# First 512 rows of x turned by TensorE instead of DMA, pinned Q/K weight loads, and memory, check and last output in smaller steps

## Chip, cores, metric

One core of one Trainium2 chip. The metric is the device time of one execution in microseconds (us), lowest is best. Only executions in the fast state are compared; the one exception is four single traces near the end (before_t1 to before_t3, pin_only_t1), for which the record leaves the state unknown and whose granted clocks (0.997 to 0.999) are those of the others. Where a "slow run" of the kernel before is spoken of below, one of its longer executions is meant (1263 us and more), which is in the fast state all the same.

Names: PE is TensorE (matmuls), PEld its weight loads, DVE is VectorE, ACT is ScalarE, POOL is GpSimd, SP is the engine whose queue issues most DMAs. "Turning" a tile means transposing it.

## The reference, cut to what matters

Two independent parts, laid side by side in the output (2048 rows, 1024 + 1024 columns, bf16).

```python
# Part A: a diagonal complex recurrence over 2048 steps between two dense projections
Bu = x @ B_bar.T            # complex, 1024 x 1024
h[t] = Lam_bar * h[t-1] + Bu[t]
y = 2 * real(hseq @ C.T) + x * Dskip

# Part B: attention in 64 segments of 32 rows, with 8 memory rows carried on
for s in range(64):
    h = concat([mem, x[32*s : 32*s+32]])       # 40 rows
    q, k, v = h @ Wq, h @ Wk, h @ Wv           # 32 heads of 128
    o = softmax(mask(q @ k.T) / sqrt(128)) @ v @ Wo
    mem, out[s] = o[:8], o[8:]
```

Part B needs x with its features on the partitions, as `b_xe` (128 partitions, 8 chunks of features, rows of x). The kernel guesses the memory rows instead of running the segments in series, computes everything at once, and checks the guess near the end. All this is the same before and after.

## The kernel before: what the change touches

The first rows of x are brought in turned, by DMA transposes on the SP queue, in pieces between the pieces of the first V weights:

```python
b.load_wv_part(w0, 0, 0, 128, nc.scalar)
b.load_xp(64, 0, 128)             # dma_start_transpose, 128 rows of x into b_xe
b.load_xp(64 + 128, 128, 128)
b.load_wv_part(w0, 0, 128, 256)
b.load_wv_part(w0, 0, 256, 512)
b.load_xp(64 + 256, 256, 128)
b.load_xp(64 + 384, 384, 128)
wv = {0: w0, 1: b.load_wv(1)}
b.load_x(1)                        # rows 512 to 1023, one DMA transpose
...
loads = [lambda: a.load_x(1), lambda: b.load_x(2), lambda: a.load_x(2),
         lambda: b.load_x(3), lambda: a.load_x(3)]   # one before each of the next V blocks
```

The first V block multiplies the four tiles of 128 rows by the first 512 columns of Wv, then copies four PSUM banks to `b_vst`, alternately on DVE and ACT, and stores `b_vst` into the DRAM tensor `b_vx`. There are two `b_vst` buffers, so a V block may only be copied out when the store of the block before the last one has landed.

```python
for i, c0, c1 in ((0, 0, 128), (1, 0, 128), (0, 128, 256), (1, 128, 256),
                  (0, 256, 512), (1, 256, 512), (2, 0, 512), (3, 0, 512)):
    self.v_mm(ps[i], w, i, c0, c1)
```

In this stage the order of PE and SP is pinned to the program's order. DVE, ACT and POOL have no pin: there the build places instructions where it expects them to fit.

```python
G.affine_select(out=k.fmask[:, 0, :], ...)     # POOL
G.memset(k.fmask[0:M, 0, :], 1.0)              # POOL
V.tensor_scalar(k.fmask[:, 1, :], k.fmask[:, 0, :], 1.0, 1.0e9, ALU.subtract, ALU.mult)   # DVE
```

## Time and profile before

| | before |
|---|---|
| time at the prediction | 1260.4 us, three runs 1260.22 to 1263.92 |
| execution that was traced | 1263.59 us (span 1261.9) |
| PE busy | 1240.1 us, 98% |
| DVE, ACT, POOL busy | 53%, 21%, 22% |

The page of the kernel before: its span, its busy line (busy us, share of the span, instructions) and the lines of the chain of waits that ended last.

```profile
span 1261.9 us, 19979 instructions
...
PE 1240.1 (98%) x8206; PEld 660.1 (52%) x8278; DVE 667.7 (53%) x1244; ACT 262.1 (21%) x629; POOL 273.8 (22%) x407
...
PE psP L62 9%; DVE c_ss L780 0%; PE psR L62 0%; DVE b_ost L89 0%; ACT b_ost L87 0%
...
```

PE is nearly always busy and the chain holds hardly anything but matmuls (it goes back only to 1145 us, hence the 9%). A microsecond is won only where PE idles or runs at half clock. The PE timeline shows where. Columns: start, duration, engine, line, operation, output and inputs, shape, count; in brackets the idle time before it and who ended it.

```profile
...
5.31 0.62 PE L62 MATMUL psP<-b_wv,b_xe 128*128 128x128 bf16 x8 [0.45 <-DMA b_xe<-in_B_x_dram]
6.61 0.62 PE L62 MATMUL psP<-b_wv,b_xe 128*128 128x128 bf16 x8 [0.68 <-DMA b_xe<-in_B_x_dram]
7.81 1.60 PE L62 MATMUL psP<-b_wv,b_xe 128*128 128x128 bf16 x16 [0.58 <-DMA b_wv<-in_B_Wv_dram]
...
15.82 0.18 PE L62 MATMUL psR<-ident,a_r 24*128 24x24 bf16 x1
16.76 0.34 PE L62 MATMUL psR<-ident,b_xr 8*128 8x8 bf16 x8 [0.76 <-DVE a_raw L168]
17.03 19.21 PE L62 MATMUL psP<-b_wv,b_xe 128*128 128x512 bf16 x86
36.81 1.89 PE L62 MATMUL psP<-b_wv,b_xe 128*128 128x512 bf16 x8 [0.57 <-ACT b_vst L87]
...
43.65 7.08 PE L62 MATMUL psP<-b_wv,b_xe 128*128 128x512 bf16 x31 [1.50 <-DMA b_xe<-in_B_x_dram]
...
```

The first three V pieces wait for DMA. `a_raw` and `b_m0` (16.76) share one PSUM bank, psR. At 36.81 PE waits for an ACT copy, and at 43.65 for the DMA transpose of block 2 of x.

The full timeline of the same trace around 350 us:

```profile
...
338.17 1.60 POOL L300 DMA_DIRECT2D a_xn<-in_A_x_dram  x3
...
341.25 0.37 ACTq L470 DMA_DIRECT2D b_vx<-b_vst  x1
...
344.39 0.38 SPq L62 DMA_DIRECT2D b_wq<-in_B_Wq_dram  x1
344.87 1.21 SPq L62 DMA_DIRECT2D b_wk<-in_B_Wk_dram  x1
...
351.80 1.58 ACT L87 ACTIVATE b_vst<-psP 128x512 bf16<-128x512 f32 x3 [6.26 <-DMA b_vx<-b_vst]
352.45 3.18 PE L62 MATMUL psP<-b_wv,b_xe 128*128 128x512 bf16 x8 [2.37 <-ACT b_vst L87]
...
```

The ACT copy at 351.80 stood 6.26 us behind a store of `b_vx`; that store is the one issued at 341.25. PE waited 2.37 us for the copy, and its next eight matmuls took 3.18 us where eight take 1.89. Between them, SP issued the Q and K weights (1 MB). For the list of waits of all engines, one line is worth keeping in mind; it cost nothing in this kernel:

```profile
...
DVE f_mask L899 <- POOL f_mask L898: 1.8, 1, 1.8
...
```

And the end of the timeline: last DVE copy, last ACT copy, last store.

```profile
...
1255.74 0.42 DVE L89 CAST b_ost<-psP 128x256 bf16<-128x256 f32 x1 [6.42 <-PE psP L62]
1256.19 0.38 ACT L87 ACTIVATE b_ost<-psP 128x256 bf16<-128x256 f32 x1 [6.46 <-DVE b_ost L89]
1256.61 0.34 ACTq L719 DMA_DIRECT2D out_dram<-b_ost  x1
```

Below, an "excess" is a number that I worked out: the time from the start of one matmul to the start of the next, less the time that the first one streams (0.216 us for 512 columns, measured in the same trace). It includes the drain that the timeline's idle column leaves out.

### The profile page before, as it was taken

Reading aid. Unit: us, or ns where it says so; the run is one execution under the profiler, and the core shown is the slowest. Engines: PE = TensorE matmul, PEld = TensorE weight load, DVE = VectorE, ACT = ScalarE, POOL = GpSimd, SP = SyncE. Lnnn points to the kernel's source line nnn. Section 1 sums busy time; section 2 is a strip of 40 time slices with the busy share of each in tenths; the row PEclk is TensorE's granted clock in tenths of the full one; section 3 lists DMA queues with packets and bytes.
Section 4 is the critical chain, followed back from the end, with each engine's and each line's share of the span. In section 5 each row is a group of like instructions: output and inputs, shape, how many; then the busy total and the mean of one; then the engine's idle time right before and its main releaser. Section 6 shows DMA issues by size and latency. Waiting matters only on the chain. (4 is left out here: it accounts for less than half of the span.)

```text
span 1261.9 us, 19979 instructions
## 1 busy us (share of the span) xinstructions
PE 1240.1 (98%) x8206; PEld 660.1 (52%) x8278; DVE 667.7 (53%) x1244; ACT 262.1 (21%) x629; POOL 273.8 (22%) x407
## 2 busy tenths in 40 slices
PE   8999999999999999999999999999999999999997
PEld 4444444444445545656566656555566554445443
DVE  3578899998711124666666666666666641001000
ACT  4344344443310000121112121211111210000000
POOL 3111331122322220232322232232222320000000
PEclk9999999999999999999999999999999999999999
DMA  9994434554898929245464544736374279407000
GB/s 236 199 234 151 142 105 129 156 144 113 224 307 260 277 80 254 64 91 129 105 145 105 140 104 104 141 77 138 94 155 97 57 212 234 90 17 151 17 25 19
DMA packets 318536, 174.18 MB, mean 138 GB/s; under 512 B 142824, under 2 KB 304352, under 8 KB 318440
## 3 DMA queue, kind: packets, MB, share of 16 engines
q1 hardware_dynamic: 296056, 146.09, 48.8%
q10 hardware_dynamic: 21360, 23.60, 6.0%
q0 software_dynamic: 1024, 3.17, 0.8%
q8 instruction: 66, 1.08, 0.4%
q14 instruction: 30, 0.25, 0.1%
HBM read 86.42 MB, written 52.19 MB: 110 GB/s over the span
## 5 line engine op out<-in xcount | busy, mean ns | idle before, releaser
L62 PE MATMUL psP<-b_xe,b_wq 128*128 128x480 bf16 (+1 forms) x1280 | 247.8, 342 | 0.0
L62 PE MATMUL psP<-b_xe,b_wk 128*128 128x480 bf16 (+1 forms) x1280 | 247.7, 343 | 0.0
L62 PE MATMUL psP<-b_wv,b_xe 128*128 128x512 bf16 (+2 forms) x1033 | 226.7, 376 | 7.1 <-ACT b_vst L87 2.9
L614 POOL TENSOR_TENSOR b_m<-b_e,maskB 99x396 bf16<-99x396 bf16 x160 | 139.6, 872 | 337.2 <-ACT b_e L611 337.2
L611 ACT ACTIVATE b_e<-psS 99x396 bf16<-99x396 f32 x176 | 88.3, 502 | 536.8 <-PE psS L62 530.7
L62 PEld LDWEIGHTS <-b_xe 128*128 128x128 bf16 x1056 | 103.0, 99 | 128.1 <-issue 5.8
L62 PEld LDWEIGHTS <-b_wk 128*128 128x128 bf16 x1280 | 119.5, 98 | 94.4
L62 PEld LDWEIGHTS <-b_wq 128*128 128x128 bf16 x1280 | 118.8, 98 | 89.4
L89 DVE CAST b_q<-psP 128x480 bf16<-128x480 f32 (+1 forms) x192 | 98.2, 533 | 97.2 <-PE psP L62 96.2
L89 DVE CAST b_k<-psP 128x480 bf16<-128x480 f32 (+1 forms) x192 | 98.0, 532 | 95.1 <-PE psP L62 95.1
L62 PEld LDWEIGHTS <-b_ol 128*128 128x128 bf16 x832 | 81.2, 98 | 97.5
L62 PE MATMUL psU<-a_xT,a_bt 128*128 128x512 bf16 x493 | 113.9, 379 | 1.5 <-DMA a_xT<-in_A_x_dram 0.5
L62 PE MATMUL psP<-t,a_hl 128*128 128x512 bf16 x497 | 111.7, 379 | 0.8
L89 DVE CAST b_ost<-psP 128x512 bf16<-128x512 f32 (+1 forms) x17 | 11.2, 661 | 190.6 <-PE psP L62 189.5
L62 PE MATMUL psP<-t,b_ol 128*128 128x512 bf16 x408 | 91.8, 379 | 0.4
L62 PE MATMUL psP<-wo,b_ol 128*128 128x512 bf16 x407 | 91.8, 379 | 0.4
L87 ACT ACTIVATE b_vst<-psP 128x512 bf16<-128x512 f32 x126 | 72.4, 592 | 89.7 <-PE psP L62 72.4
L276 POOL TENSOR_SCALAR a_tt<-a_pr,a_tabf 128x1 f32<-128x1 f32 x48 | 34.1, 710 | 248.2 <-DVE a_pr L271 248.2
L631 DVE TENSOR_TENSOR b_ob<-psO,b_accR 99x384 bf16<-99x384 f32 x160 | 85.8, 553 | 2.5
L263 DVE TENSOR_TENSOR a_pr<-psU,a_tabf 128x2048 f32<-128x2048 f32 x32 | 73.1, 2283 | 18.6 <-PE psU L62 16.9
L62 PEld LDWEIGHTS <-a_bt 128*128 128x128 bf16 x512 | 49.2, 98 | 58.2 <-DMA a_xT<-in_A_x_dram 0.5
L62 PEld LDWEIGHTS <-a_hl 128*128 128x128 bf16 x512 | 49.2, 98 | 57.1
(192 smaller groups left out, 959.4 us busy)
## 6 DMA issues: line engine op xcount, KB each, us to landing
b_v<-b_vx SPq DMA_DIRECT2D x16, 1064.2 KB
b_wv<-in_B_Wv_dram SPq DMA_DIRECT2D x16, 1024.0 KB
b_on<-b_ob SPq DMA_DIRECT2D x15, 960.0 KB
b_vx<-b_vst ACTq DMA_DIRECT2D x24, 516.0 KB
a_hs<-a_h SPq DMA_DIRECT2D x32, 256.0 KB
b_wq<-in_B_Wq_dram SPq DMA_DIRECT2D x16, 512.0 KB
b_wk<-in_B_Wk_dram SPq DMA_DIRECT2D x16, 512.0 KB
b_wog<-in_B_Wo_dram SPq DMA_DIRECT2D x4, 2048.0 KB
```

The costliest lines, as they stand in the source:

```text
L62: r = f(*a, **kw)
L87: self.S.activation(out, in_, ACT.Copy)
L89: self.V.tensor_copy(out, in_)
L263: V.tensor_tensor(pr[:], u[:].unsqueeze(1).to_broadcast([128, 2, 2, TB]), view(t3, [[TB + 1, 2], [TB + 1, 2], [1, TB]]), ALU.mult)
L276: G.tensor_scalar(tt[:, j:j + 1], w[:, j, TB - 1:TB], t3[:, 1, TB:TB + 1], None, ALU.mult)
L611: k.S.activation(e[:], s[0:GW], ACT.Exp, scale=float(E) ** -0.5, accum_out=self.accE[0:GW, i:i + 1])
L614: k.G.tensor_tensor(m[:, 0:4 * GW].rearrange("p (a b q) -> p a b q", a=2, b=2), e[:], mask[0:GW, :, :].unsqueeze(2).to_broadcast([GW, 2, 2 ...
L631: V.tensor_tensor(self.ob[:, b0:b0 + n, :], o[0:GW, 0:n, 0:E], r.unsqueeze(2).to_broadcast([GW, n, E]), ALU.mult)
```

## The change

Intent: load the first 512 rows of x plain and turn them on PE, so that the slow DMA transposes at the start fall away; keep the Q/K weight loads from being issued too early; and break up three pieces of work on which PE waited for another engine. The core of the diff:

```diff
+    def load_x0(self, tmp, i):
+        self.x0.append(tmp.tile([128, D], BF16, name="b_xr", bufs=4))
+        self.k.SP.dma_start(self.x0[i][:], self.x[0][64 + 128 * i:192 + 128 * i, :])
+
+    def turn_x0(self, i):
+        k = self.k
+        if i % 2 == 0:
+            self.xt = k.ps("U", (128, 2, KC, 128), BF16)
+        for c in range(KC):
+            k.PE.transpose(self.xt[:, i % 2, c, :], self.x0[i][:, c * 128:(c + 1) * 128], k.ident[:])
+        for h in range(2):
+            cs = slice(4 * h, 4 * h + 4)
+            k.copy("vs"[h], self.xe[:, cs, 128 * i:128 * i + 128], self.xt[:, i % 2, cs, :])
...
-            ps = [k.ps("P")[:] for _ in range(3)] + [k.ps("U", (128, 2, 512))[:, 0, :]]
-            for i, c0, c1 in ((0, 0, 128), (1, 0, 128), ...):
-                self.v_mm(ps[i], w, i, c0, c1)
+            ps = [k.ps("P")[:] for _ in range(3)]
+            self.turn_x0(0)
+            self.turn_x0(1)
+            for i, c in ((0, 0), (0, 1), (1, 0), (1, 1)):
+                self.v_mm(ps[i], w, i, 128 * c, 128 * c + 128)
+            self.turn_x0(2)
+            self.v_mm(ps[0], w, 0, 256, 512)
+            self.v_mm(ps[1], w, 1, 256, 512)
+            self.turn_x0(3)
+            ps.append(k.ps("U", (128, 2, 512))[:, 0, :])
+            self.v_mm(ps[2], w, 2)
+            self.v_mm(ps[3], w, 3)
...
-        pm = k.ps("R")
+        pm = k.ps("U", (128, 2, 512))[:, 0, :]          # init: no longer the bank of a_raw
...
-                self.k.SP.dma_start(w[:], self.Wf[i][:, :, hp * 256:(hp + 1) * 256])
+                self.k.tc.keep_in_program_order(self.k.SP.dma_start(w[:], ...))
...
-            loads = [lambda: a.load_x(1), lambda: b.load_x(2), ...]
+            loads = [lambda: b.load_x(2), lambda: a.load_x(1), ...]
...
     # v_mem and check become generators with a yield between their PE steps:
-                if i in (27, 29):
-                    b.v_mem((i - 27) // 2, wv[(i - 27) // 2])
+                if i in (26, 28):
+                    vm = b.v_mem((i - 26) // 2, wv[(i - 26) // 2])
+                if 26 <= i < 30:
+                    next(vm)
...
+    def out_last(self, ol):          # last 128 rows: columns 512, then 256, then 256
+        ...
+            k.copy("vsv"[i], ot[:, c0:c1], p[:, 0:c1 - c0])
+            k.SP.dma_start(self.out[0, T - 128:T, D + c0:D + c1], ot[:, c0:c1])
```

Also: an early Exp on ACT, the constants (with the identity) ahead of the small parameter loads, other buffers for two small tiles, and the check between the matmuls of the third block of the output projection instead of after the second.

More of the change, by code (lines that the diff above doesn't have):

```diff
@@ L101, in consts @@
     k.hpb = c.tile([128, 1], FP32, name="hpb")
+    k.hpe = c.tile([128, 1], FP32, name="hpe")
     V.memset(k.hpb[:], HALF_PI)
+    k.S.activation(k.hpe[:], k.hpb[:], ACT.Exp)
     k.ind = c.tile([128, 4], BF16, name="ind")
@@ L355, in load_m0 @@
     def load_m0(self, tmp):
-        self.m0 = tmp.tile([M, D], BF16, name="b_xr", bufs=4)
+        self.m0 = tmp.tile([M, D], BF16, name="a_h", bufs=2)
         self.k.G.dma_start(self.m0[:], self.mem0[0])
@@ L456, in v_x @@
         if first:
-            ps = [k.ps("P")[:] for _ in range(3)] + [k.ps("U", (128, 2, 512))[:, 0, :]]
-            for i, c0, c1 in ((0, 0, 128), (1, 0, 128), (0, 128, 256), (1, 128, 256), (0, 256, 512), (1, 256, 512), (2, 0, 512), (3, 0, 512)):
-                self.v_mm(ps[i], w, i, c0, c1)
+            ps = [k.ps("P")[:] for _ in range(3)]
[10 more added lines that the diff above has]
+            self.v_mm(ps[3], w, 3)
         for i in range(4):
@@ L524, in v_mem @@
         k.copy("v", vm[:], p[:, 0:4 * NM].rearrange("p (h n) -> p h n", h=4))
+        yield
         pt = k.ps("P", (128, 1024), BF16)
@@ L532, in v_mem @@
         k.SP.dma_start(self.vt[hb][:], sv[NMX:NM, :])
+        yield
     def qk_init(self, pool):
@@ L550, in load_wqk @@
                 w = self.wq.tile([128, KC, 256], BF16, name=f"b_w{'qk'[i]}{hp % 2}", bufs=1)
-                self.k.SP.dma_start(w[:], self.Wf[i][:, :, hp * 256:(hp + 1) * 256])
+                self.k.tc.keep_in_program_order(self.k.SP.dma_start(w[:], self.Wf[i][:, :, hp * 256:(hp + 1) * 256]))
                 self.wqk[hp].append(w)
@@ L713, in out_fin @@
         t = 4 * tb + tt
-        if t == TT - 1:
-            ou = self.out[0, t * 128:(t + 1) * 128, D:2 * D]
-            for i in range(2):
-                cs = slice(half * 512 + i * 256, half * 512 + i * 256 + 256)
-                k.copy("vs"[i], osts[tt][:, cs], p[:, i * 256:i * 256 + 256])
-                (k.SP, k.nc.scalar)[i].dma_start(ou[:, cs], osts[tt][:, cs])
-            return
         k.copy("s" if half else "v", osts[tt][:, half * 512:(half + 1) * 512], p[:])
@@ L744, in outproj_first @@
             self.out_fin(p, 0, tt, half, osts)
+    def out_last(self, ol):
+        k = self.k
+        ot = self.p4a.tile([128, D], BF16, name="b_ost", bufs=4)
+        for i, (c0, c1) in enumerate(((0, 512), (512, 768), (768, 1024))):
+            p = k.ps("P")
+            for h in range(H):
+                k.PE.matmul(p[:, 0:c1 - c0], ol[h][:, 384:512], self.wo[c0 // 512][:, h, c0 % 512:c0 % 512 + c1 - c0], start=(h == 0), stop=(h == H - 1))
+            k.copy("vsv"[i], ot[:, c0:c1], p[:, 0:c1 - c0])
+            k.SP.dma_start(self.out[0, T - 128:T, D + c0:D + c1], ot[:, c0:c1])
+            yield
     def outproj(self, tb, ol):
@@ L749, in outproj @@
         for tt in range(4):
+            if 4 * tb + tt == TT - 1:
+                yield from self.out_last(ol)
+                return
             for half in range(2):
@@ L764, in check @@
             k.SP.dma_start_transpose(self.omT[:, 8 * q:8 * q + 8, :], self.tn[q][:])
+        yield
         sq = pool.tile([128, 2, KC, NM], FP32, name="c_sq", bufs=1)
@@ L782, in check @@
         V.memset(onef[:], 1.0)
+        yield
         pd = k.ps("R")
@@ L918, in warm @@
 def warm(k, pool):
-    w = pool.tile([128, 512], BF16, name="b_xr", bufs=4)
+    w = pool.tile([128, 512], BF16, name="a_n", bufs=1)
     k.V.memset(w[:], 0.0)
@@ L958, in kernel_main @@
             b.load_wv_part(w0, 0, 0, 128, nc.scalar)
-            b.load_xp(64, 0, 128)
-            b.load_xp(64 + 128, 128, 128)
-            b.load_wv_part(w0, 0, 128, 256)
-            b.load_wv_part(w0, 0, 256, 512)
-            b.load_xp(64 + 256, 256, 128)
-            b.load_xp(64 + 384, 384, 128)
+            b.x0 = []
+            for i in range(4):
+                b.load_x0(p1, i)
+                if i in (1, 2):
+                    b.load_wv_part(w0, 0, 128 * i, (256, 512)[i - 1])
             wv = {0: w0, 1: b.load_wv(1)}
             b.load_x(1)
+            consts(k)
             a.load_params(p1)
             b.load_m0(p1)
-            consts(k)
             b.stage_init()
@@ L978, in kernel_main @@
             a.tables(0)
-            loads = [lambda: a.load_x(1), lambda: b.load_x(2), lambda: a.load_x(2), lambda: b.load_x(3), lambda: a.load_x(3)]
+            loads = [lambda: b.load_x(2), lambda: a.load_x(1), lambda: a.load_x(2), lambda: b.load_x(3), lambda: a.load_x(3)]
             sx = b.sum_x(p1)
@@ L1065, in kernel_main @@
                 k.SP.dma_start(wo0[:], b.Wo[:, :, 0:512])
-            if u == 4 and hp % 2 == 0 and 2 < hp + 2 < HP:
-                b.v_mem(hp // 2 + 1)
+            if hp % 2 == 0 and 2 < hp + 2 < HP:
+                if u == 4:
+                    vm = b.v_mem(hp // 2 + 1)
+                if u in (4, 6):
+                    next(vm)
             if hp == 13 and u in (3, 6, 9):
@@ L1096, in kernel_main @@
                     k.pin.add("PE")
+                if tb == 1:
+                    ck = b.check()
+                    next(ck)
                 for n, _ in enumerate(b.outproj(tb, ol)):
@@ L1099, in kernel_main @@
                         hint(k)
-                if tb == 1:
-                    for _ in b.check():
-                        pass
+                    if tb == 2:
+                        next(ck, None)
                 ol = nx
```

## The prediction

> **What bounds the kernel.** TensorE. In the page's busy table PE is busy 1240.1 of 1261.9 us (98%), and the chain of waits that ended last is almost only matmuls. In the timeline warm 128x512 matmuls start every 0.216 us. So only PE idle time, and slow-clock time after it, can be won. From the PE start times, the gaps (us over the stream time):
>
> - head, 0 to 17: DMA waits 0.86, 0.84, 0.74, 0.44 (b_xe, b_wv); half-rate matmuls from 8.1 to 11.5; 0.91 because the one psR bank must be read (a_raw) before b_init uses it;
> - 35.9: 0.73 (ACT b_vst, held by a b_vx store); 41.8: 1.66 (DMA b_xe, block 2); 71.7: 0.60 (DMA a_xT);
> - 349.7: 2.53 (ACT b_vst, which waits 6.3 us for a b_vx store), then six matmuls at 0.41 to 0.43 us and a slow b_og: 1.7 more. The Trainium skill, "TensorE: Matmul & The Clock Gate", Part 1, says that an idle array falls to half clock; this trace agrees;
> - 464.8 and 473.7: 0.72 each (transposes of b_vm wait for its DVE copy);
> - 1022 to 1030: 1.3 (psO); 1146: 1.1 (check waits for DVE c_ss, 2.24 us);
> - tail: DVE copy 0.42, then ACT copy 0.38, then the store.
>
> **What the change saves, in us.**
>
> 1. Pinned Q/K loads: 4.0. The first pair (1 MB) is now hoisted to 344.4, when DMA moves 342 GB/s and the b_vx store of 341.25 is in flight; pinned, it goes to about 430. "DMA: Bandwidth & Descriptors", Queues, rings and completion order, says that queues share each DMA engine in turn; so the store should land some us sooner, and the gap with its half-clock tail should go.
> 2. Head: 1.0 (−0.5 to 2.5). Two 128-row DMA transposes hold the SP queue 2.9 us, the next two 4.1; plain loads about 0.5 each. The bytes are the same (2 MB by about 10 us). 32 turns at 0.056 cost 1.8 of PE, plus copies of about 0.5; smaller DMA waits pay for these. The psR wait of 0.91 goes (other bank).
> 3. SP queue some 4 us ahead, and b_xe block 2 before a_xT block 1: 1.6 at 41.8, 0.4 at 35.9 and 71.7 together. Block 2's issue should come at about 21, not 30.
> 4. Memory V in two steps: 1.4.
> 5. Check between other matmuls: 1.0.
> 6. Last output: one copy fewer in series, 0.4; 64 matmuls of 256 columns cost 0.1 more: 0.3.
> 7. Early Exp and constants: nothing, but the identity must be ready for the turns.
>
> Sum 9.7; less about 0.8 for new collisions: 8.9. All lies on PE's stream.
>
> **Prediction: 1251.5 us (1247.0 to 1257.0, 8 in 10). Faster by over 2%: 0.01; within 2%: 0.98; slower by over 2%: 0.01.**
>
> **What would show it.** PE waits: no ACT b_vst wait near 345, no half-rate matmuls there, b_wq/b_wk issued near 430 (1); second v block starting by 16 instead of 17.0 (2); no b_xe wait near 40 (3); no b_vm and c_ss waits on PE (4, 5); one copy after the last matmul (6). PE's own busy sum should hardly fall.
>
> **What would make it wrong.** Identity or x tile late: PE idles, falls to half clock and the head loses 1 to 2 us. The store at 341 limited by the 3 MB that POOL issues from 335, not by Q/K: step 1 gives under 1. A pinned weight load holding up the in-order SP queue in the attention stage: new PE waits between 500 and 1030.

## The result, and the profile after

Ratios here are the mean time of one kernel's fast runs over that of the other kernel's fast runs of the same rounds, so they are not quite the ratio of the medians quoted.

| | before | after |
|---|---|---|
| median of 4 runs | 1262.16 us | 1260.74 us |
| lowest to highest | 1260.22 to 1264.28 | 1259.40 to 1262.23 |
| ratio (95% interval) | | 0.9989 (0.9964 to 1.0013) |
| execution that was traced | 1263.59 us | 1259.40 us |

The class was foreseen (within 2%), the size was not: 8.9 us were expected, and the interval holds between 4.5 us won and 1.6 us lost. The page of the kernel after:

```profile
span 1257.7 us, 20118 instructions
...
PE 1239.0 (99%) x8270; PEld 664.0 (53%) x8342; DVE 668.2 (53%) x1248; ACT 263.7 (21%) x633; POOL 273.4 (22%) x407
...
```

PE's waits, longest in total first (columns: engine and what it wanted, who ended the wait, us in total, times, longest):

```profile
...
PE psU L62 <- ACT b_xe L87: 6.2, 2, 5.1
PE psU L62 <- DMA a_xT<-in_A_x_dram: 1.6, 1, 1.6
...
```

The waits on `b_vst`, `b_vm`, `c_ss` and `b_xe` that were to go are gone. A new one stands in front: 6.2 us for the ACT copy of a turned tile. The full timeline of the kernel after shows what is behind it:

```profile
...
9.03 0.61 PE L62 MATMUL psU<-ident,b_xr 128*128 128x128 bf16 x8
...
9.47 1.91 PE L62 MATMUL psP<-b_wv,b_xe 128*128 128x256 bf16 x16
...
15.13 0.12 POOL L936 MEMSET f_mask<- 8x40 f32 x1
15.29 0.18 DVE L937 TENSOR_SCALAR f_mask<-f_mask 40x40 f32<-40x40 f32 x1 [7.62 <-POOL f_mask L936]
15.38 0.41 DVE L89 COPY b_xe<-psU 128x512 bf16<-128x512 bf16 x1
...
15.82 0.60 ACT L87 ACTIVATE b_xe<-psU 128x512 bf16<-128x512 bf16 x1 [7.53 <-DVE b_xe L89]
...
16.47 1.01 PE L62 MATMUL psU<-ident,b_xr 128*128 128x128 bf16 x8 [5.09 <-ACT b_xe L87]
...
17.70 3.19 PE L62 MATMUL psP<-b_wv,b_xe 128*128 128x512 bf16 x7 [0.22 <-issue]
...
20.69 2.51 PE L62 MATMUL psU<-b_wv,b_xe 128*128 128x512 bf16 x8
...
```

The third turn is done at 9.64 us. Its DVE copy runs at 15.38. DVE did nothing in between: it stood at `f_mask`, which waits for the last of POOL's mask instructions (15.13). The ACT copy of that tile follows the DVE copy, the fourth turn follows the ACT copy, and PE idles 5.09 us. After that it runs at half clock: the turns start every 0.107 us instead of 0.056, and the ten matmuls from 17.70 on every 0.427 us instead of 0.216. The Trainium skill, "TensorE: Matmul & The Clock Gate", Part 1, says that an idle array falls to half clock and needs some microseconds of work to get back; this trace agrees, with 5.1 us of idling before and 5.5 us of half rate after (16.47 to 21.96). At 346 us, on the other hand, the store is no longer waited for by PE:

```profile
...
346.37 0.37 ACTq L496 DMA_DIRECT2D b_vx<-b_vst  x1
346.88 1.59 POOL L302 DMA_DIRECT2D a_xn<-in_A_x_dram  x3 [3.71 <-ACT b_vst L87]
...
353.16 1.09 ACT L87 ACTIVATE b_vst<-psP 128x512 bf16<-128x512 f32 x2 [2.50 <-DMA b_vx<-b_vst]
...
```

And the end has one copy after the last matmul:

```profile
...
1252.95 0.42 DVE L89 CAST b_ost<-psP 128x256 bf16<-128x256 f32 x1 [6.24 <-PE psP L62]
```

Following the same matmuls through both traces gives the change of each stretch:

| start of | before | after | change in the stretch |
|---|---|---|---|
| parameter matmul (end of first V block) | 15.82 | 23.13 | +7.31 |
| second V block | 17.03 | 23.44 | −0.90 |
| first block of part A | 38.53 | 44.21 | −0.73 |
| second block of part A | 50.56 | 54.57 | −1.68 |
| fourth block of part A | 72.29 | 77.41 | +1.12 |
| output projection of part A | 356.76 | 357.70 | −4.18 |
| first Q projection | 481.64 | 481.09 | −1.49 |
| last attention matmul | 1030.23 | 1028.50 | −1.18 |
| end of last matmul | 1255.70 | 1252.91 | −1.06 |
| end of span | 1261.89 | 1257.71 | −1.40 |

So in this pair of traces 12.6 us were won and 8.4 given back, 7.3 of that within the first V block.

### The profile page after: what moved, and what is told of

It is laid out like the page before. It is cut to its first block, busy times and chain, and to the rows that moved or that the text cites. A ratio compares the mean times of both kernels' runs of the same rounds, so it can differ in the third digit from the quotient of the medians.

```text
span 1257.7 us, 20118 instructions
## 1 busy us (share of the span) xinstructions
PE 1239.0 (99%) x8270; PEld 664.0 (53%) x8342; DVE 668.2 (53%) x1248; ACT 263.7 (21%) x633; POOL 273.4 (22%) x407
## 4 chain that ended last, share of the span: by engine, by line
PE 96%; POOL 1%; DMA 1%; DVE 1%; issue 1%; ACT 0%; SPq 0%; POOLq 0%; ACTq 0%; DVEq 0%
PE psP L62 80%; PE psU L62 9%; PE psS L62 3%; PE psO L62 2%; PE psR L62 2%; DMA a_xT<-in_A_x_dram 1%; POOL b_m L642 0%; DVE a_pr L273 0%; DVE a_pr L265 0%; POOL a_r L163 0%; ACT b_e L639 0%; DVE a_n L284 0%; DVE a_pr L268 0%; POOL maskB L123 0%; POOL maskA L123 0%
## 5 line engine op out<-in xcount | busy, mean ns | idle before, releaser
L62 PEld LDWEIGHTS <-b_ol 128*128 128x128 bf16 x864 | 84.2, 98 | 94.5
L62 PE MATMUL psP<-wo,b_ol 128*128 128x512 bf16 (+1 forms) x440 | 91.9, 364 | 0.4
```

The source lines that it names most:

```text
L62: r = f(*a, **kw)
```

## The experiments

Theories for the head. A: the order on DVE, where `f_mask` stands ahead of a copy on which PE now depends. B: the fourth tile of x lands late. C: two turns share one PSUM tile, so a turn waits for the copies of the turn before it by dependency alone.

The trace speaks against B already (PEld loads the fourth tile at 11.12 us), and the order as built shows how A can come about. DVE's order, counted from its first instruction, in the kernel after and in the same kernel with `f_mask` on POOL:

```
after                                   f_mask on POOL
 7 TensorCopy  b_xe<-psU                 7 TensorCopy  b_xe<-psU
 8 TensorCopy  a_jf<-a_k                 8 TensorCopy  a_jf<-a_k
 9 TensorCopy  b_xe<-psU                 9 TensorCopy  b_xe<-psU
10 TensorScalar f_mask<-f_mask          10 TensorCopy  b_xe<-psU
11 TensorCopy  b_xe<-psU                11 TensorCopy  b_vst<-psP
12 TensorCopy  b_vst<-psP               12 TensorCopy  b_xe<-psU
```

The Trainium skill, "TensorE: Matmul & The Clock Gate", in the specification table at its top, calls the queues of VectorE, ScalarE and GpSimd strict first-in first-out. This trace agrees: the copy was ready at 9.64 us and started at 15.38, right behind `f_mask`.

### e1: f_mask on GpSimd

```diff
-    V.tensor_scalar(k.fmask[:, 1, :], k.fmask[:, 0, :], 1.0, 1.0e9, ALU.subtract, ALU.mult)
+    G.tensor_scalar(k.fmask[:, 1, :], k.fmask[:, 0, :], 1.0, 1.0e9, ALU.subtract, ALU.mult)
```

> The kernel after, with the one VectorE instruction f_mask (40x40) done on GpSimd. Theory A (in-order VectorE): in the kernel after, f_mask stands in VectorE's order ahead of the b_xe copy of the third turned tile, waits for GpSimd's masks until 15.29 us and so holds the turn of the fourth tile, the first V block and its half-clock tail. Then here the 5.4 us gap of PE at 11.1 us is gone, the second V block starts at 17 to 18.5 us instead of 23.4, and the time falls by 3 to 6 us against the kernel after, so 0.993 to 0.996 of before. Theory B (the fourth x tile lands late, DMA): gap and time as in the kernel after. Theory C (the pair of turns shares one psU tile, so turn 4 waits for the copies of turn 3 by dependency alone): gap falls to about 1.3 us as between turns 1 and 2, so A and C agree here and the next run tells them apart.

Measured: 1255.33 us (1251.72 to 1259.02, 6 runs), ratio 0.9946 (0.9921 to 0.9972). In the timeline the copy of the third tile follows its turn, and the second V block starts at 17.04 us instead of 23.44:

```profile
...
11.19 0.42 DVE L89 COPY b_xe<-psU 128x512 bf16<-128x512 bf16 x1 [2.77 <-PE psU L62]
...
12.73 0.61 PE L62 MATMUL psU<-ident,b_xr 128*128 128x128 bf16 x8
...
13.40 1.67 PE L62 MATMUL psP<-b_wv,b_xe 128*128 128x512 bf16 x7
...
15.39 0.38 POOL L937 TENSOR_SCALAR f_mask<-f_mask 40x40 f32<-40x40 f32 x1
...
17.04 3.19 PE L62 MATMUL psP<-b_wv,b_xe 128*128 128x512 bf16 x14
...
```

One 40x40 instruction off DVE, and the gap of 5 us is gone. That fits A and C, not B. Of the 6.4 us won in the head the trace gives 2.1 back near 70 us: there PE waits 1.9 us for `a_xT`, and half-rate matmuls follow.

### e2: a PSUM tile for each turn

```diff
-        if i % 2 == 0:
-            self.xt = k.ps("U", (128, 2, KC, 128), BF16)
+        xt = k.ps("U", (128, 2, KC, 128), BF16)          # written and read at index 0 only
```

> The kernel after, with a psU tile of its own for each turn; f_mask stays on VectorE. Theory A: the fourth turn no longer waits, but the third block's copies still stand behind f_mask until 15.3 us and matmuls of tile 2 need them, so PE still idles some 4.5 us at 11 to 16 us and the time is within 1 us of the kernel after. Theory C: the long gap goes, the second V block starts at 17 to 18.5 us, and the time falls by 3 to 6 us. Both: the 1.3 us gap between turns 1 and 2 at 5.2 us shrinks to 0.6 or less.

Measured: 1258.86 us (1257.82 to 1259.33), ratio 0.9974 (0.9952 to 0.9995). The fourth turn runs without waiting, and then PE waits all the same, for the DVE copy itself:

```profile
...
PE psP L62 <- DVE b_xe L89: 4.6, 1, 4.6
...
```

C is out as the cause of the long gap: the wait only moved by one instruction. C does hold for the short one: the 1.14 us between the first two turns went. The time is 1.8 us below the kernel after in the same rounds (1260.62), where A expected less than 1. The chain f_mask, DVE copy, PE is the cause of the long gap.

### The two kernels again

> The kernel before itself, for noise and for a second trace. Its four runs fell in two groups, near 1260.3 and near 1264.1. If the groups are the PE gap at 349.7 us with its half-clock tail (4.2 us, waiting for a b_vx store), a run near 1260 shows no such gap, or a short one, and one near 1264 shows it. If the gap stands in both groups, they come from elsewhere (clock or start). Ratio to before 1.000 within 0.002.

> The kernel after itself, for a second trace and a narrower interval. Theory A: the gap of 5 us at 11.1 us stands in every trace, because the order on VectorE is fixed at build time. Ratio to before 0.997 to 1.000.

Measured: before against itself 1.0009 (0.9984 to 1.0034), its runs from 1259.73 to 1268.02 us. The kernel after against before 0.9987 (0.9965 to 1.0009), runs from 1258.69 to 1260.87, and the wait for ACT `b_xe` is there again (6.1 us in total). The second trace of before, of its slowest run (1268.02), has a wait of 4.1 us for `b_xe` block 2 where the first trace had 1.5, and again 2.1 us for `b_vst` near 354 us.

### e4: the kernel before, only with the Q/K loads pinned

```diff
-                self.k.SP.dma_start(w[:], self.Wf[i][:, :, hp * 256:(hp + 1) * 256])
+                self.k.tc.keep_in_program_order(self.k.SP.dma_start(w[:], self.Wf[i][:, :, hp * 256:(hp + 1) * 256]))
```

> The kernel before with nothing but the pinned Q/K loads. If the hoisted 1 MB of Q/K weights makes the b_vx store late, PE's wait for ACT b_vst near 350 us (2.5 and 2.3 us in two traces of before) goes, the eight matmuls after it start every 0.216 us, and the time falls by 4 us: 0.9968 of before (0.995 to 0.999). If the store is late because of GpSimd's 3 MB alone, the wait stays above 1.5 us and the time does not change.

Measured: 1261.43 us (1258.24 to 1264.77), ratio 0.9999 (0.9977 to 1.0022). The timed runs show no gain, and exclude 4 us. Yet the timeline shows that the pin does what it should:

```profile
...
345.16 0.37 ACTq L470 DMA_DIRECT2D b_vx<-b_vst  x1
...
353.98 1.58 ACT L87 ACTIVATE b_vst<-psP 128x512 bf16<-128x512 f32 x3 [4.54 <-PE psP L62]
354.63 1.89 PE L62 MATMUL psP<-b_wv,b_xe 128*128 128x512 bf16 x8 [0.65 <-ACT b_vst L87]
...
```

PE waits 0.65 us instead of 2.37, and the next eight matmuls take 1.89 us instead of 3.18. What was wrong with my 4 us? Both traces of before were of slow runs. So I took three more traces of before and one more of the pin alone.

> The kernel before, one more trace. Theory R (the spread of before is the wait for b_xe block 2 near 41 us alone): every trace shows the b_vst wait of about 2.3 us near 350 us, and the times differ as the wait near 41 us does (1.7 to 4.5 us). Theory S (the wait near 350 us comes and goes too): a run near 1259 to 1260 us shows less than 1 us there, and then pinning the Q/K loads gains nothing in such runs, which would explain why the timed runs of the pin alone did not fall.

> The same question of Theory R or S as for the trace beside it: does the wait for ACT b_vst near 350 us (2.3 us) stand in every run of before, or less than 1 us in its fast runs.

> The same question of Theory R or S, a third trace: does the wait for ACT b_vst near 350 us (2.3 us) stand in every run of before, or less than 1 us in its fast runs.

> The kernel before with the pinned Q/K loads alone, a second trace: wait for ACT b_vst near 350 us below 1 us and no half-rate matmuls after it, in the fast as in the slow runs; a wait for b_xe near 41 us of 0 to 4.5 us that decides the time.

| trace | time us | excess near 41 us | near 70 us | near 350 us | from 6th block of part A to its output projection |
|---|---|---|---|---|---|
| before, first | 1263.59 | 1.66 | 0.60 | 2.53 | 262.93 |
| before_again | 1268.02 | 4.30 | 1.25 | 2.26 | 262.65 |
| before_t1 | 1259.28 | none | 0.78 | 2.18 | 260.93 |
| before_t2 | 1259.74 | none | 1.60 | 2.08 | 260.83 |
| before_t3 | 1260.52 | none | 1.99 | 1.98 | 260.73 |
| pin alone | 1264.21 | 4.48 | none | 0.81 | 259.56 |
| pin alone, second | 1260.97 | none | 2.19 | 1.03 | 259.78 |
| after | 1259.40 | none | 1.72 | none | 258.76 |

The timeline of before_t1 near 350 us:

```profile
...
338.86 0.63 ACT L272 ACTIVATE a_g<-a_pr 128x512 bf16<-128x512 f32 x1
...
341.99 0.38 SPq L62 DMA_DIRECT2D b_wq<-in_B_Wq_dram  x1
...
349.06 1.58 ACT L87 ACTIVATE b_vst<-psP 128x512 bf16<-128x512 f32 x3 [5.90 <-DMA b_vx<-b_vst]
349.71 1.89 PE L62 MATMUL psP<-b_wv,b_xe 128*128 128x512 bf16 x8 [2.01 <-ACT b_vst L87]
...
```

Neither theory was quite right. The wait for `b_vst` is in every trace of before (so S falls), but the half-rate matmuls after it are only in the two slower ones: here eight matmuls take 1.89 us right after the wait. And the wait near 41 us is in the slow runs only. So Theory R is right in part: the stretch with block 2 (first to second block of part A) makes 1.7 of the 3.7 us by which the first trace is longer than the fast ones, and 6.8 of the 8.2 us of before_again, where half-rate matmuls follow the gap. The half-rate stretch after 350 us makes most of the rest (2.1 and 1.8 in the table's last column). Against the fast traces, the last column's means say that the pin alone is worth 260.83 − 259.67 = 1.2 us; against the slow ones, 3.1. The interval of the timed runs allows the 1.2 and not the 4.0.

### e8: the pin undone on a quiet base

This and the next two runs start from e6 (below): the kernel after with both repairs and earlier loads.

> The run with both repairs and the loads together, with the Q/K loads not pinned. Undoing step 1 alone on a base whose runs lie within 1.6 us. If the hoisted Q/K loads hold up the b_vx store, b_wq and b_wk are issued near 335 us, PE waits 1.5 to 2.5 us for ACT b_vst near 340 us, half-rate matmuls follow, and the time is 1252 to 1254 us. If the store is limited by GpSimd's loads alone, the time stays at 1249 to 1250.

Measured: 1249.37 us (1249.32 to 1250.26); e6, on another chip, had 1249.20, and the stretch of the table's last column takes 258.75 us in both traces. No PE wait for `b_vst`, although Q was issued at 339.19 us again (K only at 345.53, so this is half of the burst). On this base the pin is worth nothing measurable. The other thing that differs between the runs with a wait and those without is when POOL issues the 0.75 MB of `a_xn`: about 3 us ahead of the `b_vx` store in all traces with the old head (338.17 against 341.25 in the first), 0.5 us behind it in all traces with the turned head (346.88 against 346.37 in the kernel after, where POOL waited 3.71 us for an ACT copy of `b_vst`). The wait near 350 us is 0.8 to 2.5 us in the nine traces of the first kind and absent in the nine of the second. The Trainium skill, "DMA: Bandwidth & Descriptors", section on queues, rings and completion order, says that each DMA engine takes packets from its queues in turn; that a store lands sooner with less queued beside it agrees: from the store's issue to the copy that it released took 10.55 us (before), 9.04 (pin alone, second) and 6.79 (after). That the later `a_xn` is the cause was not tried by itself; why the turned head moves it is open as well.

### e5, e3, e6, e7: the head, and a version that beats both

e5 is the kernel after with the old head: DMA transposes and the old order of the first V block, all else changed.

> The kernel after with the old head (first 512 rows of x by DMA transpose, no turns); all else of the change stays, f_mask too. If the turned head is where the gain went, the first V block ends at 15.5 to 16 us, the second starts at 16 (psR wait gone), no VectorE or ScalarE wait of PE before 40 us, and the time is 1251 to 1255 us, 0.991 to 0.995 of before. If the gain was lost elsewhere (pins, load order), it stays near 0.998.

Measured: 1253.10 us (1252.26 to 1259.15), ratio 0.9944 (0.9922 to 0.9967). First V block done at 15.13 us; the second starts at 16.69, not at 16 as expected, because PE waits 1.2 us for `b_wv`. So the rest of the change gives its gain, and the turned head as written takes it back.

e3 has both repairs, `f_mask` on GpSimd and a PSUM tile for each turn.

> f_mask on GpSimd and a psU tile for each turn. Against the run with f_mask alone the PE wait of 1.2 us between turns 1 and 2 shrinks to 0.6 or less and the half-clock stretch at 6 to 10 us gets shorter; the first V block ends at 15 to 16.5 us instead of 16.7. Time 0 to 1.5 us below that run. The wait for a_xT near 70 us (2 us) stays, so part of it is given back there.

Measured: 1253.05 us (1251.53 to 1255.83), ratio 0.9937 (0.9918 to 0.9955). First V block done at 14.52 us, 2.2 us earlier than in e1 and 1.3 earlier than before; expected were 15 to 16.5. The time is 2.3 us below that of e1, but e1 ran on another chip in other rounds; by the two ratios it is about 1.1, within the 0 to 1.5 that were expected. As expected, part of it came back as a wait for `a_xT` near 70 us (2.3 us). The SP timeline of e1 shows why that load is late: it stands behind the store of `a_h`, which waits for DVE.

```profile
...
60.61 0.33 SPq L62 DMA_DIRECT2D a_hs<-a_h  x1
60.98 6.83 SPq L62 DMA_TRANSPOSE a_xT<-in_A_x_dram  x1
...
```

e6 is e3 with that load moved ahead in the program:

```diff
-loads = [lambda: b.load_x(2), lambda: a.load_x(1), lambda: a.load_x(2), lambda: b.load_x(3), lambda: a.load_x(3)]
+loads = [lambda: b.load_x(2), lambda: a.load_x(1), lambda: (a.load_x(2), b.load_x(3), a.load_x(3))]
```

> The run with both repairs, and the three DMA transposes b_xe block 3 and a_xT blocks 2 and 3 issued together, one V block earlier for the first and two for the last, ahead of the a_hs stores that wait for VectorE. If the wait for a_xT near 70 us is only the in-order SP queue standing behind those stores (the load is issued at 61 us right after one), the wait goes and the time falls 2 to 4 us below the run with both repairs: 1250 to 1253 us. If it is DMA throughput, the wait moves to 40 to 50 us and nothing is won.

Measured: 1249.20 us (1249.11 to 1250.70), ratio 0.9909 (0.9890 to 0.9928). It beats both kernels and is 3.9 us below e3 in the same rounds. The traces show where: the wait near 70 us (an excess of 2.5) is gone, and so are the half-rate matmuls behind it (from the fourth to the fifth block of part A 12.31 us in e3, 10.76 in e6). Its runs lie within 1.6 us where those of before in the same rounds spread over 6.6. PE's waits, all that are left in the span:

```profile
...
PE psR L62 <- DVE hpb L103: 1.3, 1, 1.3
PE psO L62 <- POOL b_m L641: 0.8, 3, 0.4
PE psP L62 <- ACT b_xe L87: 0.2, 1, 0.2
```

e7 is e5 with the same earlier loads.

> The old head with all else of the change and the three loads issued together; against the run with both repairs and those loads (1249.2 us) only the head differs. If the turned head, once repaired, is worth the 1.0 us that was predicted for it, this takes 1250 to 1252.5 us (first V block 0.5 to 1 us later, psR wait gone in both, perhaps a b_vst wait near 350 us). If the head is worth nothing, 1248.5 to 1249.8.

Measured: 1251.88 us (1250.54 to 1253.18), against 1249.37 for e8 on the same chip. In the traces, the first V block of e7 is done at 15.57 us, that of e6 at 14.88; 0.8 more is a `b_vst` wait near 346 us. So the repaired head is worth 0.7 us within the first V block, near the 1.0 that was predicted for it, and 1.5 in the traces with the wait that goes along with it. The medians differ by 2.5 us; the traced run of e7 is one of its shorter ones, and the rest was not followed up.

### e9 and e10: the order of loads, and the small steps

e9 puts a_xT block 1 before b_xe block 2 again:

> The same base, with a_xT block 1 before b_xe block 2 again. If the order is what step 3 is worth, PE waits 0.5 to 4 us for b_xe near 38 to 40 us as in the traces of before (1.5 and 4.1), the spread of the runs grows, and the time is 1250 to 1253 us. If the SP queue being ahead is enough, the time stays at 1249 to 1250.

Measured: 1250.85 us (1250.58 to 1251.31), 1.5 us above e8 in the same rounds; PE waits 1.3 us for `b_xe` near 39 us. The spread did not grow. So the order is worth 1.5 us here; being ahead on the SP queue is not enough.

e10 undoes the two steps of memory V, the spread check and the last output on the same base.

> The same base, with memory V in one step, the check in one piece and the last output as before. Predicted: b_vm 1.4 and c_ss 1.0 us of PE waits come back; last output 0.3 by the prediction, about 1.4 by the traces, where the end of the program after the last store's issue took 5.3 us before and 4.3 after. So 1251.9 us by the prediction, 1253 by the traces.

Measured: 1255.47 us (1254.95 to 1257.04), 6.1 us above e8 where 2.5 to 3.6 were expected; its trace is 5.5 us longer than that of e6. By stretches: 1.5 for the first two memory V, 1.15 in the attention stage, 1.8 from the last attention matmul to the last matmul, with the check (0.76 of it a PE gap among the check's matmuls that the kernel before does not have; the trace names no releaser for it, and its cause is open), 1.3 after the last matmul. The first 347 us were 0.3 shorter. The 1.15 us are six gaps of 0.18, one at each memory V of the attention stage; I had not seen them in the profile because each is so short.

## Why the prediction was wrong

| step | predicted saving, us | what the runs showed |
|---|---|---|
| 1 pinned Q/K loads | 4.0 | 1.2 by the pin alone against fast traces of before, 3.1 against slow ones; the wait went wholly only together with later a_xn loads |
| 2 head | 1.0 (−0.5 to 2.5) | −6.4 in the pair of traces (+7.31 and −0.90); +0.7 once repaired |
| 3 SP ahead, order of loads | 1.6 and 0.4 | 2.4 up to 51 us, of which 1.1 is lost again near 72; none in fast runs of before, which have no such wait; 1.5 for the order on the quiet base |
| 4 memory V | 1.4 | 1.5, and 1.2 more in the attention stage |
| 5 check | 1.0 | about 1.1 (end of last matmul −1.06, with step 6's longer matmuls inside it) |
| 6 last output | 0.3 | about 1.3 (end of span −1.40, less 0.1 for the matmuls) |
| 7 Exp and constants | 0 | none seen |

The step that failed is step 2: "Head: 1.0 (−0.5 to 2.5) ... 32 turns at 0.056 cost 1.8 of PE, plus copies of about 0.5". The turns cost what was said: in the trace of e3 they start every 0.056 us. The copies took 0.42 us on DVE and 0.60 on ACT, but one of them could not start for 5.7 us, because DVE was held by `f_mask`. e1 shows this. The second V block, forecast "by 16", started at 23.44. I had priced the copies by their duration, as if DVE were free at that moment. The two copies of a tile also do not overlap: in the traces of the kernel after, e1, e2, e3 and e6 the ACT copy starts only when the DVE copy has ended, so a tile takes about 1.05 us and not 0.5 (why they do not overlap was not tested). That is the 1.14 us between the first two turns. The profile of before had shown the wait that did it: "DVE f_mask L899 <- POOL f_mask L898: 1.8, 1, 1.8". There nothing on PE depended on DVE until 15.9 us, so the wait cost nothing. The change puts PE behind that queue. That the build would place `f_mask` ahead of the third tile's copy stands in no profile of before, but it can be read in the built order of the kernel after without a run. "Identity or x tile late" was named as a danger, with 1 to 2 us; the form was right (PE idles, then half clock), the cause and the size were not.

Beside it, steps 1 and 3 were sized from one trace, and that was of a run of 1263.59 us, while the time to be lowered was 1260.4. The half-rate stretch after 350 us and the wait near 41 us belong to the slow runs; three traces of runs near 1260 us have neither. That took away nearly 2 of step 1 and most of step 3. The danger named for step 1, that POOL's loads limit the store, may have come true in part: the pin alone gives 1.2 of the 2.1 us that the kernel after wins there over fast runs of before, and what gives the rest was not tested by itself. In the other direction, steps 4 and 6 were underrated. The sums meet: against the three fast traces of before the kernel after gains 2.1 near 350 us, 2.7 at memory V, 1.1 at the check and 1.4 at the end, 7.3 together; the head takes 6.6 of it and the stretch up to the sixth block of part A 0.3. That leaves about 0.45, as the traced times do (1259.85 in the mean against 1259.40). The medians differ by 1.1 to 1.4, because they hold the slow runs of before too.

What was right: PE bounds the kernel; the busy sum hardly fell (1240.1 to 1239.0); no wait for `b_vst`, `b_vm`, `c_ss` or `b_xe` block 2; and no new wait in the attention stage from the pinned loads. "Block 2's issue should come at about 21" was right too: 21.78.

## What to carry to other kernels

When a change gives a waiting engine's queue new work that the bottleneck depends on, read what stands ahead of that work in the queue and when it is released; a harmless wait on an idle engine becomes a critical one. Size a saving from a trace whose time is that of the median run, or from two or three traces: here one trace of a slow run doubled the expected gain of one step and made up most of that of another. And when a good idea measures as nothing, follow the same instruction through both traces; gains and a single loss lie next to each other there.

## What the Trainium skill lacked or had wrong

- "TensorE: Matmul & The Clock Gate", Part 4, says that in transpose mode the full clock does not engage, and gives 275 to 390 ns for a 128x128 turn. Here turns start every 0.056 us while PE is warm (0.219 us each), as fast as matmuls of 128 columns, and every 0.107 us after the 5 us gap. They follow the clock like the other matmuls here; whether turns alone would bring the full clock is not shown.
- The same page, "Why this matters for your kernels", advises against PE gaps over about 3 us. Gaps with an excess of 2.3 and 2.5 us were followed by half-rate matmuls (0.41 to 0.43 us instead of 0.216), gaps of 2.0 to 2.2 us in the same place were not, in five traces. Near 70 us gaps of 2.1 (e1), 2.2 (e5 and the second trace of the pin alone) and 2.5 us (e3) were followed by half rate and one of 2.3 us (e2) was not. So gaps well under 3 us can cost the full clock, and these runs give no sharp limit.
- "Runtime: NRT & Kernel Launch" prices the runtime's own steps after a kernel, but neither it nor another page that I read mentions this part of a program's end, which the trace's semaphore records show: SP checks some twenty semaphores one after the other, about 0.07 us each. Where the first of them belongs to the last store, all come after it (before: last store issued at 1256.61 us, span end 1261.89, 5.3 us); where it is the last of its kind, most are done while the store flies (after: issued at 1253.40, end 1257.71, 4.3 us). By these records that is why one store on SP instead of two on SP and ACT saved about 1 us more than the copy; e10, with the old last output, has the old end again (5.3 us from its last store's issue), e6 the new one (4.4).
